# Spreading eight experts' weight loads, moving sends earlier, and regrouping the outer steps in a long convolution with routed experts

## The chip, the cores and the metric

The kernel runs on one core of one Trainium2 chip. The metric is the device time of one execution in microseconds (us), lower is better. The engines are TensorE (PE for matmuls, PEld for weight loads), VectorE (DVE), ScalarE (ACT), GpSimd (POOL) and SyncE (SP), which here issues nearly all direct DMAs and computes nothing.

## The reference

```
def _attn_ref(x, v, pos_emb, w1, w2):             # x, v: 4 x 11456 x 128
    h_filt = (np.maximum(pos_emb @ w1, 0) @ w2) * window
    y = irfft(rfft(x * v, n=2*S) * rfft(h_filt, n=2*S))[:, :S]
    return x * y
def _moe_ref(x, modality_id, w_gate, modality_bias, w1, w2):   # x: 45824 x 128
    logits = x @ w_gate + modality_bias[modality_id]           # 8 experts
    e_idx = argmax(logits); gate_w = softmax(logits)[e_idx]
    for e in range(8):                                         # w1[e]: 128 x 1024
        out[mask] = gate_w[mask] * (relu(x[mask] @ w1[e]) @ w2[e])
```

A long convolution over the sequence (by a transform of length 2S, a product, the inverse transform) is multiplied by x; each of the 45824 rows that result goes to its one best expert, a two-layer network of 128 to 1024 to 128.

## The kernel before

**Convolution and routing, about the first half of the span.** For each batch b of four there is an outer stage and a middle stage. An outer stage has 16 steps q, and each does the forward transform of a piece of batch b (`forward`, matmuls `s` of L464, copied to `A` by ACT) and, for batch b−1, the inverse transform: `turn0` and `turn1` transpose four 128x128 blocks each into PSUM twice (tile `wt`, L662), and ACT copies each `wt` out (L663); `inverse` makes `py` (L671), ACT copies half of it (L674), DVE adds, subtracts and multiplies by x. Every second step the routing of eight tokens a position goes on: `half` transposes the result (`xT`, L707), `logits` is the product with the gate (`pl`, L718), `lturn` turns that back (`lt`, L727), `biased` and `choice` find the best expert on DVE, and `send` counts the rows per expert by three matmuls (`pr`, `pn`, L785 to L790) and makes row numbers from `pr` and `pn` on DVE (L792, L793). The middle stage has 23 groups: products in the frequency domain (`pz`, L596, DVE and POOL on `part` and `more`) and inverse matmuls (`pw`, L639).

What runs in which order is a table. `OUTER` names the functions; the number behind a name is its delay in steps, and the place in the string is its order inside a step. `OV` is the number of outer steps that are interleaved with the first middle groups, `EM` says how many steps before the outer stage's end the middle stage's first step goes. PE, ACT, DVE and SP run their instructions in the order in which the program writes them; POOL's order is made by a scheduler. PSUM tiles are taken in turn: single banks (`wt`, `xT`, `pl`, `pr`, `pn`, `lt`) from four, pairs (`py`, `s1`, `pz`) from two.

**Sends.** `send_rows(1)` scatters 128 finished rows into the experts' regions of the buffer `xs` (L269, an indirect DMA on POOL). They start in the middle stages, and those of the last batch go on in the first half of the experts.

**Experts, the second half.** 82 full tiles of 512 rows in eight steps c, then half tiles of 256 rows in four steps (those beyond tile 98 lie in a branch that is skipped). Per step `hidden` is three matmuls (L1105 to L1107: high parts of weights and rows, and the two low parts), ACT's relu (L1110) and DVE's low part of it (L1111); `result` is three matmuls into `po` (L1128 to L1130), three steps late. `weights(i + 1, c)` splits the next tile's expert weights into a high part (ACT, L1064) and a low part (DVE, `wl`, L1065), in four pieces. SP's queue has, at c = 0 of tile i, `rows_in(i + 2)`: four loads of `x` (L1004), one of `ends` (gate and row number, L1006), and for tiles 0 to 7 the tile's own expert weights `w1r` and `w2r` (0.5 MB each, L1027, L1029). From tile 8 on the weights come from `w1a` and `w2a`, which hold all eight experts: 16 loads of 0.5 MB, the eight of `w1a` issued in one go in `rows_in(6)` and the eight of `w2a` in `rows_in(7)` (L1039, L1042). At the end of a tile its result goes through DRAM to change its layout: `ob<-oT` (four DMAs, L1140), then `y<-ob` (L1142), which waits for them. `rows_out` multiplies by the gate on POOL (`ot`, L1157) and scatters 128 rows at a time to `out` (L1159). `rows_turn` transposes `x` on DVE (`xT`, L1082) and casts the row numbers (`idx`, L1083), `rows_split` makes `xh` (ACT, L1091) and `xl` (DVE, L1092).

From tile 50 on the generator `rest` writes one tile of empty rows behind each expert's region (SP, `xs<-pad`, L952), each after all scatters that were issued before it, and makes the tables of the later tiles, among them those of the half tiles.

Of the kernel before, what the change touches and what calls it, by code (L numbers as in the profile page):

```python
# [12 lines left out]
F32 = mybir.dt.float32  # L13
# [8 lines left out]
ENG = mybir.EngineType  # L22
# [13 lines left out]
B, S, D, E, F = 4, 11456, 128, 8, 1024  # L36
# [4 lines left out]
NQ = N2 // 4  # L41
NO = N2 // 8
NC = 16
T = 512
# [4 lines left out]
def surely_full(n):  # L49
# [5 lines left out]
NH = (N - T * NF - E) // TH + E  # L55
RW = D + 2
NOWHERE = 1 << 20
OUTER = ("turn0:1 turn1:1 lturn:3 biased:3 forward:2 load_x:0 product:1 half:2 choice:3 "
         "inverse:1 logits:2 send:4 shift:2 load:0 store:4 places:5")
LAST = ("lturn:5 biased:5 send:6 turn0:1 choice:5 turn1:1 inverse:2 logits:4 half:3 shift:4 load_x:0 store:5 places:6")  # L60
FOUT = "load:0 hidden:2 transform:3"
FMID = "turn:0 spectrum:1 second:3"
FIRST = "forward:17 load:0 product:16"
MID = "load_c:2 spectrum:2 inverse:4 load:0"
OV, EA, EM = 2, 3, 4
F1, F2, F3 = 1, 18, 1
UNSURE = 5
TG, FL = 18, 2
NDYN = 8
# [110 lines left out]
def hyena_moe_kernel(ctx: ExitStack, tc: tile.TileContext, a: dict, out: bass.AP,  # L180
# [180 lines left out]
    with ExitStack() as cv:  # L361
# [451 lines left out]
        def outer_steps(b):  # L813

            by_block = lambda name, f: {f"{name}{k}": lambda q, k=k: f(q, k) for k in (0, 1)}
            todo = {}
            if b > 0:
                load_x, turn, itransform = inverse_stages(b - 1)
                rturn, logits, lturn, shift, biased, choice, send, store, places = route_stages(b - 1)
                todo = {  # L820
                    "load_x": load_x, **by_block("turn", turn), "inverse": itransform,
                    "half": lambda q: rturn(q // 2, q % 2), "logits": every_other(logits),
                    "lturn": every_other(lturn), "shift": every_other(shift),
                    "biased": every_other(biased),
                    "choice": every_other(choice), "send": every_other(send),
                    "store": every_other(store), "places": every_other(places)}
            if b < nb:
                load, product, transform = forward_stages(b)
                todo |= {"load": load, "product": product, "forward": transform}
            if b == nb:  # L830
                todo.pop("places")
                for name in ("half", "logits", "lturn", "biased", "choice"):
                    todo[name] = but_last(todo[name], 2)
                todo["send"] = but_last(todo["send"], 4)
                todo["store"] = but_last(todo["store"], 6)
                o = NO - 1
                finale.extend([
                    lambda late: (store(o - 2), store(o - 1), rturn(o, 0, late)),
                    lambda late: (send(o - 1), rturn(o, 1, late)), lambda late: None,
                    lambda late: logits(o, late), lambda late: None,  # L840
                    lambda late: (lturn(o), biased(o, late)), lambda late: (choice(o), store(o)),
                    lambda late: None, lambda late: (send(o), places(o))])
            table = [w.split(":") for w in (LAST if b == nb else OUTER if b else FIRST).split()]

            if 0 < b < nb:
                later.append([lambda f=todo[n]: f(NQ - 1) for n in ("store", "places")])
                todo["store"] = but_last(todo["store"], 2)
                todo.pop("places")
            return steps(NQ, [(lambda q, t=int(t): min(q + t, NQ + 3) if 0 < b < nb else q + t, todo[n])
                              for n, t in table if n in todo])  # L850

        def early(first, second, n):
# [115 lines left out]
        yield from tile_table(new, tabs["3"], took, start, left, NH, TH)  # L968

    outs, fetched = [], []  # L970
    kept = {}
    second, others = second_table(), rest()
    NCH = F // D
# [6 lines left out]
    def experts(lo, hi):  # L980
# [5 lines left out]
        def rows_in(i):  # L986
            if i > last:
                return
            tb, col, n = tiles[i]
            for gen in {"1": (), "b": (second,)}.get(tb, (second, others)):  # L990
                for _ in gen:
                    pass
            tab = tabs[tb]
            r = nc.values_load(tab[0:1, 0, col:col + 1], engines=[ENG.SP], min_val=0, max_val=E * R,
                               skip_runtime_bounds_check_because="clamped above")
            k = kept[i] = {"n": n}

            x = k["x"] = mt.tile([D, T // 32, 32], F32, tag="x", name="x", bufs=4)
            ends = k["ends"] = mt.tile([D, 4, 2], F32, tag="ends", name="ends", bufs=8)

            def rows():

                of = xs[ds(r, n), 0:D].rearrange("(f t) (k e) -> k t f e", t=32, e=32)
                lds = [sp.dma_start(x[32 * j:32 * j + 32, 0:n // 32], of[j]) for j in range(4)]  # L1004
                way = "(j p) r -> p j r" if i == last else "(p j) r -> p j r"
                lds.append(sp.dma_start(ends[:, 0:n // D],  # L1006
                                        xs[ds(r, n), D:RW].rearrange(way, j=n // D)))
                if tb in ("1", "b"):

                    known = max(nb - (2 if tb == "1" else 1), 0) * NR // D  # L1010
                    assert len(scatters) >= known
                    for ld in lds:
                        for s in scatters[known:]:
                            tc.declare_no_dep(ins_of(ld), s, reason="rows of later tiles")
                        after_all(ld, scatters[:known])

            def raw_weights():

                e = nc.values_load(tab[0:1, 2, col:col + 1], engines=[ENG.SP], min_val=0, max_val=E - 1,
                                   skip_runtime_bounds_check_because="clamped above")  # L1020
                k["w", 0] = mt.tile([D, F], F32, tag="w1r", name="w1r")
                k["w", 1] = mt.tile([D, NCH, D], F32, tag="w2r", name="w2r")
                w1 = a["moe_w1"][ds(e, 1)].rearrange("e p f -> p (e f)")
                w2 = a["moe_w2"][ds(e, 1)].rearrange("e (c p) d -> p (e c) d", p=D)
                cuts = 2 if i == 0 else 1
                cut = lambda h, n: slice(h * n // cuts, (h + 1) * n // cuts)
                return [lambda h=h: sp.dma_start(k["w", 0][:, cut(h, F)], w1[:, cut(h, F)])  # L1027
                        for h in range(cuts)] + [
                    lambda h=h: sp.dma_start(k["w", 1][:, cut(h, NCH)], w2[:, cut(h, NCH)])  # L1029
                    for h in range(cuts)]  # L1030

            of = raw_weights() if i < NDYN else []
            for part in of[:1] + [rows] + of[1:] if i == 0 else [rows] + of:
                part()
            if i < NDYN:
                k["w", 1] = k["w", 1].rearrange("p c d -> p (c d)")
            if i == min(NDYN, last) - 2:
                for e in range(E):
                    sp.dma_start(w1a[:, e], a["moe_w1"][e])  # L1039
            if i == min(NDYN, last) - 1:  # L1040
                for e in range(E):
                    sp.dma_start(w2a[:, e], a["moe_w2"][e].rearrange("(c p) d -> p c d", p=D))  # L1042

        def weights(i, part):

# [3 lines left out]
            tb, col, _ = tiles[i]  # L1049
            if part == 0 and i >= NDYN:  # L1050
                k["e"] = nc.values_load(
                    tabs[tb][0:1, 1, col:col + 1], engines=[ENG.Activation, ENG.DVE], min_val=0,
                    max_val=(E - 1) * F, skip_runtime_bounds_check_because="clamped above")
            if part % 2 == 0:
                m = part // 2
# [6 lines left out]
            else:  # L1062
                src = wv[m][:, ds(k["e"] + at, half)]
            act.copy(k[m, "h"][:, at:at + half], src)  # L1064
            dve.tensor_sub(k[m, "l"][:, at:at + half], src, k[m, "h"][:, at:at + half].bitcast(F32))  # L1065

        def turn_tiles(i):

# [6 lines left out]
        def rows_turn(i):  # L1075
# [4 lines left out]
            if "idx" not in k:  # L1080
                turn_tiles(i)
            dve.transpose(k["xT"][:, 0:n], k["x"].rearrange("p f e -> p (f e)")[:, 0:n])  # L1082
            dve.tensor_copy(k["idx"][:, 0:n // D], k["ends"][:, 0:n // D, 1])  # L1083

        def rows_split(i):
            if i > last:
# [57 lines left out]
        def rows_out(i):  # L1144
# [3 lines left out]
            n = k["n"]  # L1148
            ot = mt.tile([D, T], F32, tag="ot", name="ot", bufs=4).rearrange("p (j d) -> p j d", d=D)
            gate = k["ends"][:, 0:n // D, 0:1].broadcast_to([D, n // D, D])  # L1150
            if i == last:
                pt = bank("pt")
                for j in range(n // D):
# [17 lines left out]
        for at in range(len(work) + 6):  # L1171
# [7 lines left out]
                finale[at - FL](late)  # L1179
            if lo == 0 and at >= FL + len(finale) + 2 and len(waiting) <= RC and not fetched:  # L1180
                fetched.append(fetch(nb - 1))
            if lo == 0 and 2 * at % 7 < 2:
                send_rows(1)
            if 8 <= i < NW0:
                next(second, 0)
            if NW1 - 10 <= i < NW1:
# [2 lines left out]
                weights(i + 1, c)  # L1189
            result(at - 3)  # L1190
            whole = i <= last and tiles[i][2] == T
            if c == (3 if whole else 1):
                rows_turn(i + 1)
            if c == (4 if whole else 2):
                rows_split(i + 1)
            if c == (5 if whole else 3):
                rows_out(i - 1)
# [50 lines left out]
```

## Time and profile before

| what | value |
|---|---|
| median of 3 runs | 2198.53 us (2196.98 to 2200.67) |
| profiled execution, its own time | 2200.3 us |
| its span in the trace | 2198.5 us |
| mean granted TensorE clock | 0.985 |
| busy share: PE, PEld, DVE | 94%, 76%, 79% |
| busy share: ACT, POOL | 54%, 54% |
| queue q1 (SP's DMAs), share of 16 engines | 58.1% |

A busy PE is not a PE at its peak, since matmuls are pipelined; a stage is judged by its pitch, the time from one tile or step to the next. A wait in the trace stands in square brackets behind an instruction: the idle time just before it and what ended it. The busy shares are means over stages that have different limits, so each stage has to be read by itself.

### The profile page before, as it was taken

The numbers are of one execution on the slowest core, as the hardware profiler recorded it, in microseconds if no ns is written. First come the engines' busy times: TensorE is split into PE (matmuls) and PEld (weight loads), VectorE is DVE, ScalarE is ACT, GpSimd is POOL, SyncE is SP. The second block draws the span as 40 slices with busy tenths as digits, with TensorE's granted clock in tenths as the row PEclk, the third lists the DMA queues.
The fourth block names the chain that finished last, engine by engine and source line by source line (L and its number), as shares of the span: only waits on it lengthen the run. The fifth ranks groups of instructions, "written<-read, shape, count | busy, mean of one in ns | idle before, by whom it ended". The sixth has DMA issues, their size and how long they took to land. (4 is left out here: it accounts for less than half of the span.)

```text
span 2198.5 us, 50801 instructions
## 1 busy us (share of the span) xinstructions
PE 2076.5 (94%) x18024; PEld 1668.0 (76%) x18024; DVE 1736.2 (79%) x2946; ACT 1185.9 (54%) x2155; POOL 1186.4 (54%) x1130
## 2 busy tenths in 40 slices
PE   8989999899999999899987999999999999999985
PEld 8878776687767776687556788888888788888885
DVE  2349766896779867896895799888899899889884
ACT  4642366225652266324654566666666566666663
POOL 0216400496448855596425577777777455555533
PEclk9999999999999999999999899999999999999998
DMA  9576677678878788785678865666665555555432
GB/s 315 227 275 222 231 223 221 223 260 272 280 247 269 258 280 288 242 263 174 199 194 232 185 137 126 124 131 124 124 128 122 105 107 98 97 97 95 80 68 55
DMA packets 592748, 406.52 MB, mean 185 GB/s; under 512 B 455977, under 2 KB 489469, under 8 KB 592489
## 3 DMA queue, kind: packets, MB, share of 16 engines
q1 hardware_dynamic: 565833, 343.82, 58.1%
q0 software_dynamic: 26496, 59.36, 7.8%
q8 instruction: 144, 2.36, 0.5%
q14 instruction: 115, 0.94, 0.1%
q10 hardware_dynamic: 160, 0.03, 0.0%
HBM read 295.03 MB, written 108.42 MB: 184 GB/s over the span
## 5 line engine op out<-in xcount | busy, mean ns | idle before, releaser
L1111 DVE SCALAR_TENSOR_TENSOR hl<-ph,hh 128x512 fp32r<-128x512 f32 x724 | 485.6, 681 | 83.6 <-ACT hh L1110 76.4
L1110 ACT ACTIVATE hh<-ph 128x512 fp32r<-128x512 f32 x724 | 422.4, 597 | 203.6 <-PE ph L1107 197.1
L269 POOL DMA_INDIRECT xs<-back,to x360 | 375.8, 1044 | 279.1 <-DVE y L675 95.4
L1159 POOL DMA_INDIRECT out<-ot,idx x362 | 404.5, 1117 | 114.3 <-issue 80.2
L1107 PE MATMUL ph<-xl,wh 128*128 128x512 f32 (+1 forms) x792 | 298.4, 377 | 15.5 <-DVE xl L1092 15.5
L1128 PE MATMUL po<-hh,wh 128*128 128x512 f32 (+1 forms) x792 | 296.7, 375 | 13.4 <-ACT hh L1110 13.4
L1105 PE MATMUL ph<-xh,wh 128*128 128x512 f32 (+1 forms) x792 | 297.5, 376 | 11.1 <-ACT xh L1091 11.0
L1130 PE MATMUL po<-hl,wh 128*128 128x512 f32 (+1 forms) x792 | 296.9, 375 | 9.8 <-DVE off L316 5.1
L1106 PE MATMUL ph<-xh,wl 128*128 128x512 f32 (+1 forms) x792 | 296.7, 375 | 0.0
L1129 PE MATMUL po<-hh,wl 128*128 128x512 f32 (+1 forms) x792 | 295.7, 373 | 0.0
L643 ACT COPY A<-pw 128x512 f32<-128x512 f32 (+1 forms) x184 | 97.1, 579 | 346.3 <-PE pw L639 346.3
L1157 POOL TENSOR_TENSOR ot<-y,ends 128x512 f32<-128x512 f32 (+1 forms) x98 | 110.8, 1131 | 245.5 <-DMA y<-ob 238.0
L615 DVE TENSOR_TENSOR part<-pz,rings 128x1024 f32<-128x1024 f32 (+1 forms) x184 | 211.5, 1191 | 2.2 <-POOL part L620 2.2
L639 PE MATMUL pw<-rings,part 64*128 64x128 f32 x2880 | 201.1, 279 | 2.5 <-POOL part L620 2.5
L639 PEld LDWEIGHTS pw<-rings,part 64*128 64x128 f32 x2880 | 176.3, 188 | 35.7 <-issue 27.7
L610 POOL TENSOR_TENSOR more<-more 128x256 f32<-128x256 f32 (+1 forms) x92 | 73.0, 794 | 235.4 <-issue 150.0
L596 PE MATMUL pz<-A,rings 128*64 128x256 f32 x1440 | 176.2, 387 | 12.5 <-issue 7.3
L1107 PEld LDWEIGHTS ph<-xl,wh 128*128 128x128 f32 x792 | 151.2, 191 | 45.9 <-DVE xl L1092 20.0
L1128 PEld LDWEIGHTS po<-hh,wh 128*128 128x128 f32 x792 | 150.8, 190 | 40.8 <-ACT hh L1110 14.7
L1130 PEld LDWEIGHTS po<-hl,wh 128*128 128x128 f32 x792 | 150.6, 190 | 40.0 <-DVE hl L1111 8.8
L464 PE MATMUL s<-fwd,seq 128*64 128x90 f32 x4096 | 171.2, 242 | 9.2 <-issue 4.8
L1105 PEld LDWEIGHTS ph<-xh,wh 128*128 128x128 f32 x792 | 151.3, 191 | 37.5 <-ACT xh L1091 12.1
(180 smaller groups left out, 3720.5 us busy)
## 6 DMA issues: line engine op xcount, KB each, us to landing
rings<-hs SPq DMA_DIRECT2D x88, 512.0 KB
seq<-in_u SPq DMA_DIRECT2D x64, 512.0 KB
seq<-in_v SPq DMA_DIRECT2D x64, 512.0 KB
seq<-in_x SPq DMA_DIRECT2D x64, 512.0 KB
xr<-xo SPq DMA_DIRECT2D x64, 365.6 KB
back<-xr SPq DMA_DIRECT2D x72, 325.0 KB
rings<-in_c_b SPq DMA_DIRECT2D x88, 256.0 KB
rings<-in_c_c SPq DMA_DIRECT2D x88, 256.0 KB
```

The costliest lines, as they stand in the source:

```text
L269: s = pool.indirect_dma_start(out=xs, out_offset=bass.IndirectOffsetOnAxis(ap=ix, axis=0), in_=src, in_offset=None, bounds_check=E * R - 1 ...
L615: dve.tensor_mul(part[i], z[:, :, i].unsqueeze(1).broadcast_to([D, 2, n, 2, D]), h[:, 0].unsqueeze(3).broadcast_to([D, 2, n, 2, D]))
L639: pe.matmul(pw[par][:, to:to + D], t[at], k["c"][at, q, c], start=i == 0, stop=i == len(terms) - 1)
L1105: pe.matmul(p, k[0, "h"][:, f:f + D], k["xh"], start=True, stop=False)
L1106: pe.matmul(p, k[0, "l"][:, f:f + D], k["xh"], start=False, stop=False)
L1107: pe.matmul(p, k[0, "h"][:, f:f + D], k["xl"], start=False, stop=True)
L1110: act.activation(hh, ph, AF.Relu)
L1111: dve.scalar_tensor_tensor(hl, ph, 0.0, hh.bitcast(F32), op0=ALU.max, op1=ALU.subtract)
L1128: pe.matmul(po, k[1, "h"][:, f], hh[:, t], start=g == 0, stop=False)
L1129: pe.matmul(po, k[1, "l"][:, f], hh[:, t], start=False, stop=False)
L1130: pe.matmul(po, k[1, "h"][:, f], hl[:, t], start=False, stop=g == NCH - 1)
L1159: s = pool.indirect_dma_start(out=out, out_offset=bass.IndirectOffsetOnAxis(ap=k["idx"][:, j:j + 1], axis=0), in_=ot[:, j, :], in_offset=N ...
```

## The change

- The table `OUTER` is ordered anew and several delays grow by one; `OV` goes from 2 to 3, `EM` from 4 to 5, and the bound on late steps from NQ + 3 to NQ + 4.
- The 16 loads of `w1a` and `w2a` are issued one at a time, at odd c of tiles 2 to 5, `w1a` and `w2a` in turn.
- `send_rows(1)` is called in 3 of 10 steps where it was 2 of 7.
- The cast of `idx` moves from DVE in `rows_turn` to POOL in `rows_out`.
- In half tiles the low parts of two of the four weight pieces move from DVE to POOL, and `rows_turn` and `rows_split` come one step earlier.

```diff
-OUTER = ("turn0:1 turn1:1 lturn:3 biased:3 forward:2 load_x:0 product:1 half:2 choice:3 "
-         "inverse:1 logits:2 send:4 shift:2 load:0 store:4 places:5")
+OUTER = ("turn0:1 turn1:1 lturn:4 biased:4 send:5 half:3 forward:2 load_x:0 product:1 choice:4 "
+         "inverse:1 logits:3 shift:3 load:0 store:5 places:6")
-OV, EA, EM = 2, 3, 4
+OV, EA, EM = 3, 3, 5
...
-            if i == min(NDYN, last) - 2:
-                for e in range(E):
-                    sp.dma_start(w1a[:, e], a["moe_w1"][e])
-            if i == min(NDYN, last) - 1:
-                for e in range(E):
-                    sp.dma_start(w2a[:, e], a["moe_w2"][e].rearrange("(c p) d -> p c d", p=D))
+            if i == NDYN:
+                whole_weights(2 * E)
+
+        def whole_weights(n):
+            for _ in range(min(n, len(bulk))):
+                e, m = bulk.pop(0)
+                to, of = ((w1a[:, e], a["moe_w1"][e]) if m == 0 else
+                          (w2a[:, e], a["moe_w2"][e].rearrange("(c p) d -> p c d", p=D)))
+                sp.dma_start(to, of)
...
-            dve.tensor_sub(k[m, "l"][:, at:at + half], src, k[m, "h"][:, at:at + half].bitcast(F32))
+            eng = pool if k["n"] < T and part % 2 else dve
+            eng.tensor_sub(k[m, "l"][:, at:at + half], src, k[m, "h"][:, at:at + half].bitcast(F32))
...
-            dve.tensor_copy(k["idx"][:, 0:n // D], k["ends"][:, 0:n // D, 1])      # in rows_turn
+            pool.tensor_copy(k["idx"][:, 0:n // D], k["ends"][:, 0:n // D, 1])     # in rows_out
...
-            if lo == 0 and 2 * at % 7 < 2:
+            if lo == 0 and 3 * at % 10 < 3:
                 send_rows(1)
+            if lo == 0 and 2 <= i and c % 2:
+                whole_weights(1)
...
-            if c == (3 if whole else 1):
+            if c == (3 if whole else 0):
                 rows_turn(i + 1)
-            if c == (4 if whole else 2):
+            if c == (4 if whole else 1):
                 rows_split(i + 1)
```

On PE, in the outer stage, the second step of a pair before, from one `py` to the next (`ident` is the identity for transposes, `A` the transformed data, `oh` and `sc` the choice and its running count, `seq` the input):

```order
L671 MATMUL py<-rings,inv 64x512 x4
L718 MATMUL pl<-rings,wg 32x436 x4
L785 LDWEIGHTS both
L785 MATMUL pr<-oh_100,both 128x128
L787 LDWEIGHTS both
L787 MATMUL pr<-sc_102,both 128x128
L790 LDWEIGHTS both
L790 MATMUL pn<-sc_102,both 128x8
L662 MATMUL wt<-ident,A 90x128 x16
L727 MATMUL lt<-ident,lT 109x128 x4
L464 MATMUL s_4393<-fwd,seq 64x90 x16
L464 MATMUL s_4411<-fwd,seq 64x90 x16
```

The same step now:

```order
L671 MATMUL py<-rings,inv 64x512 x4
L662 MATMUL wt<-ident,A 90x128 x16
L785 LDWEIGHTS both
L785 MATMUL pr<-oh_100,both 128x128
L787 LDWEIGHTS both
L787 MATMUL pr<-sc_102,both 128x128
L790 LDWEIGHTS both
L790 MATMUL pn<-sc_102,both 128x8
L707 MATMUL xT<-ident,xo_88 128x109 x8
L464 MATMUL s_4374<-fwd,seq 64x90 x16
L464 MATMUL s_4392<-fwd,seq 64x90 x16
L671 MATMUL py<-rings,inv 64x512 x4
```

The three matmuls of `pr` and `pn` stood ahead of the 16 of `wt` and stand behind them now; `lt` has gone to the other step of the pair, and `xT` stands ahead of the forward matmuls.

On SP, in the first tiles of the experts, from the `ends` load of tile 6 before (`ob`, `y`: the layout change of a tile's result):

```order
L1006 DMA ends<-xs 128x4x2
L1027 ISA
L1027 DMA w1r<-in_moe_w 128x1024
L1029 ISA
L1029 DMA w2r<-in_moe_w 128x8x128
L1039 DMA w1a<-in_moe_w 128x1024 x8
L1140 DMA ob_70<-oT 32x16x32 x4
L1142 DMA y<-ob_70 128x512
```

The same queue in one of the tiles 2 to 5 now:

```order
L1007 DMA ends<-xs 128x4x2
L1028 ISA
L1028 DMA w1r<-in_moe_w 128x1024
L1030 ISA
L1030 DMA w2r<-in_moe_w 128x8x128
L1047 DMA w1a<-in_moe_w 128x1024
L1145 DMA ob_68<-oT 32x16x32 x4
L1147 DMA y<-ob_68 128x512
L1047 DMA w2a<-in_moe_w 128x8x128
L1047 DMA w1a<-in_moe_w 128x1024
L1047 DMA w2a<-in_moe_w 128x8x128
```

Eight loads in one go became four a tile, one ahead of the `ob` DMAs and three behind `y`.

On POOL, in the half tiles before, one after another:

```order
L1157 TENSOR_TENSOR ot<-y,ends 128x256
L1159 DMA out<-ot,idx 45824x128 x2
L1157 TENSOR_TENSOR ot<-y,ends 128x256
L1159 DMA out<-ot,idx 45824x128 x2
```

And now:

```order
L1163 TENSOR_TENSOR ot<-y,ends 128x256
L1071 ISA
L1071 TENSOR_TENSOR wl<-w1a,wh 128x512
L1165 DMA out<-ot,idx 45824x128 x2
L1156 CAST idx<-ends 128x2
L1071 ISA
L1071 TENSOR_TENSOR wl<-w2a,wh 128x512
L1056 TENSOR_LOAD tab_22019
```

Two `wl` pieces and the `idx` cast stand among the gate product and the scatters of a tile.

## Rows read from the trace of the kernel before

**Rows 1.** Windows: us; PE, PEld, DVE, ACT, POOL busy; granted clock; DMA share; GB/s.
```profile
1145.00:1178.00 33.00, 32.81 (x145) 27.06 (x145) 29.04 (x51) 22.39 (x42) 15.51 (x14) 1.00 0.73 174
...
1180.00:1190.00 10.00, 8.90 (x37) 6.43 (x37) 5.44 (x10) 4.14 (x8) 6.37 (x7) 1.00 0.97 317
...
2100.00:2150.00 50.00, 43.21 (x318) 41.58 (x319) 40.84 (x78) 31.07 (x59) 18.21 (x20) 0.93 0.37 69
```

**Rows 2.** Timeline of one pair of outer steps, all engines (start, duration, instruction).
```profile
305.68 2.00 PE L662 MATMUL wt<-ident,A 128*90 128x128 f32 x16
...
306.47 2.06 ACT L663 COPY rings<-wt 90x512 f32<-90x512 f32 x4
...
307.62 2.70 PE L464 MATMUL s<-fwd,seq 128*64 128x90 f32 x64
...
314.03 2.75 PE L662 MATMUL wt<-ident,A 128*90 128x128 f32 x16
...
316.34 0.28 DVE L792 TENSOR_TENSOR score<-pr,base 109x128 f32<-109x128 f32 x1
...
316.87 0.69 PE L727 MATMUL lt<-ident,lT 128*109 128x128 f32 x4
```

**Rows 3.** Timeline of PE where an outer stage passes into a middle stage.
```profile
394.00 1.46 PE L464 MATMUL s<-fwd,seq 128*64 128x90 f32 x32 [0.99 <-DVE y L677]
...
412.96 1.30 PE L596 MATMUL pz<-A,rings 128*64 128x256 f32 x10 [1.06 <-issue]
```

**Rows 4.** Groups of PE by line, 1300 to 1420 us (busy us, mean ns).
```profile
L1105 PE MATMUL ph<-xh,wh 128*128 128x512 f32 x89 | 34.6, 389 | 0.0
```

**Rows 5.** The same view, 1170 to 1290 us.
```profile
L1105 PE MATMUL ph<-xh,wh 128*128 128x512 f32 x69 | 28.0, 405 | 0.0
```

**Rows 6.** SP's DMA queue in the first tiles of the experts, and ACT's wait.
```profile
1180.88 5.77 SPq L1039 DMA_DIRECT2D w1a<-in_moe_w  x8
...
1207.79 0.62 ACT L1064 CAST wh<-w1r 128x512 fp32r<-128x512 f32 x1 [14.66 <-DMA w1r<-in_moe_w]
```

**Rows 7.** Timeline of SP's queue and POOL at the writes of empty rows.
```profile
1710.42 14.65 SPq L952 DMA_DIRECT2D xs<-pad  x5
...
1734.26 0.98 POOL L269 DMA_INDIRECT xs<-back,to  x1 [14.24 <-DMA xs<-pad]
```

**Rows 8.** Groups of PE by line, 1690 to 1770 us.
```profile
L1105 PE MATMUL ph<-xh,wh 128*128 128x512 f32 x54 | 21.5, 398 | 0.0
```

**Rows 9.** SP's DMA queue in the half tiles: first, a middle and last cycle.
```profile
2057.14 1.97 SPq L1140 DMA_DIRECT2D ob<-oT  x4
...
2116.62 1.86 SPq L1004 DMA_DIRECT2D x<-xs  x4
2118.67 0.55 SPq L1006 DMA_DIRECT2D ends<-xs  x1
2119.27 2.08 SPq L1140 DMA_DIRECT2D ob<-oT  x4
...
2164.24 1.97 SPq L1140 DMA_DIRECT2D ob<-oT  x4
```

**Rows 10.** Half tiles: PE by form, 2055 to 2165 us, and DVE by form, 2100 to 2150 us.
```profile
L1107 PE MATMUL ph<-xl,wh 128*128 128x256 f32 x119 | 35.9, 302 | 14.8 <-DVE xl L1092 14.8
...
L1065 DVE TENSOR_TENSOR wl<-w2a,wh 128x512 fp32r<-128x512 f32 x13 | 8.8, 680 | 0.1
...
L1083 DVE CAST idx<-ends 128x2 int32<-128x2 f32 x6 | 1.1, 185 | 0.7 <-DMA ends<-xs 0.7
```

**Rows 11.** POOL's groups by line, 1300 to 1650 us.
```profile
L269 POOL DMA_INDIRECT xs<-back,to x75 | 76.6, 1022 | 22.9 <-issue 22.3 <-DVE hl L1111 0.3 <-DVE wl L1065 0.3
L1157 POOL TENSOR_TENSOR ot<-y,ends 128x512 f32<-128x512 f32 x33 | 39.2, 1188 | 20.8 <-DMA y<-ob 20.6
```

**Rows 12.** Timeline of POOL and DVE at the end of the half tiles.
```profile
2163.12 0.61 POOL L1157 TENSOR_TENSOR ot<-y,ends 128x256 f32<-128x256 f32 x1 [3.68 <-DMA y<-ob]
...
2163.18 1.10 DVE L1065 TENSOR_TENSOR wl<-w1a,wh 128x512 fp32r<-128x512 f32 x1
```

More of the change, by code (lines that the diff above doesn't have):

```diff
@@ L848, in outer_steps @@
                 todo.pop("places")
-            return steps(NQ, [(lambda q, t=int(t): min(q + t, NQ + 3) if 0 < b < nb else q + t, todo[n])
+            return steps(NQ, [(lambda q, t=int(t): min(q + t, NQ + 4) if 0 < b < nb else q + t, todo[n])
                               for n, t in table if n in todo])
@@ L970, in hyena_moe_kernel @@
     outs, fetched = [], []
+    bulk = [(e, m) for e in range(E) for m in range(2)]
     kept = {}
@@ L1051, in weights @@
                 k["e"] = nc.values_load(
-                    tabs[tb][0:1, 1, col:col + 1], engines=[ENG.Activation, ENG.DVE], min_val=0,
+                    tabs[tb][0:1, 1, col:col + 1], engines=[ENG.Activation, ENG.DVE] + [ENG.Pool] * (k["n"] < T), min_val=0,
                     max_val=(E - 1) * F, skip_runtime_bounds_check_because="clamped above")
```

## The prediction

> **What bounds the kernel now.** I read the windows first, because the page's shares are means over stages with different limits, and then the stretches by groups and timelines.
>
> In the full expert tiles PE is the limit. The groups of PE by line show 89 first matmuls of L1105 in 120 us without a wait [rows 4], which is 1.35 us a step; six matmuls at their undisturbed pace make 1.36, so a tile of eight steps lasts 10.88 us. No part of the change shortens that; a gain can only come from stretches where this pace is lost. There are four.
>
> First, the outer stages. In one step of a pair the 16 transposes `wt` start at 305.68 and the next group at 307.62, after 1.94 us; in the other they start at 314.03 and the next group at 316.87, after 2.84 [rows 2]. The other step holds `pr` and `pn`, which were made just before and are not read until DVE's L792 at 316.34. They hold two of the four single PSUM banks, so the four `wt` groups share two and each waits for ACT's copy, some 0.52 us each (2.06 for four). 0.90 us is lost each time; there are six such places in each of three stages, 18 in all.
>
> Second, where an outer stage passes into a middle stage, PE waits in several places, among them 0.99 for DVE's y and 1.06 behind `pw` [rows 3]; I added up 7.4 us over each of the three passages against the groups' undisturbed times.
>
> Third, tiles 5 to 10. In 120 us there are 69 first matmuls, not 89 [rows 5]: 20 steps of 1.36 us, 27 us, are missing; by the tiles' starts 26.4. SP's queue says why: eight loads of `w1a` go out at 1180.88 and take 5.77 us to issue, and the next tile's own weights land so late that ACT stands 14.66 us [rows 6]. DMA engines are 0.97 busy there, at 317 GB/s, against 0.73 and 174 GB/s with the tiles' own weights alone [rows 1].
>
> Fourth, tiles 52 and 53. SP stands 14.65 us at five writes of empty rows, which wait for scatters issued before them, and POOL's next send 14.24 us for those writes [rows 7]; PE makes 54 steps in 80 us where 59 fit [rows 8].
>
> Then the half tiles: 119 matmuls of L1107, eight a tile, in 110 us [rows 10] are a pitch of 7.4 us, against 5.44 (half of 10.88) at PE's pace; there are sixteen such pitches. PE's wait there is put down to DVE's `xl`, 14.8 us in 110 [rows 10], and DVE is the nearly busy engine (40.84 of 50) [rows 1]. But SP's queue runs without a gap: `ends` goes out at 2118.67, is done by 2119.22, and `ob` of the next result follows at 2119.27; from 2057.14 to 2164.24 there are 14 such cycles, 7.65 us each [rows 9]. Had the result been late, SP would have stood ahead of `ob`. It stands instead between `ob` and `y`, for the write's landing. So SP's chain of small transfers sets this pitch, and DVE is late because its rows are.
>
> **The change part by part.** The sum starts from the profiled execution's own 2200.3 us (span 2198.5); the median is 1.8 us lower.
>
> *Outer order.* Nothing is added or removed. In the new order `wt` stands ahead of `pr` and `pn`, so their banks are no longer held, but two `xT` groups follow and take banks over from `wt`; ACT has y's copy of 0.6 us in front of its four `wt` copies. By those durations the last copy ends 2.85 us after the group starts, and `xT` ends 0.40 later than PE alone would have it. I take 0.90 − 0.40 = 0.5 us, × 18 = 9 us. Bounds: no stall left, 16; the same stall under another name, 0; a regrouping that starves DVE of its pairs, −9.
>
> *Passages (OV, EM).* One more outer step is laid among middle groups. The waits of 0.99 and 1.06 get other work ahead of them and go; `send`'s wait of about one for the choice stays. 7.4 falls to about 5.9, 1.5 × 3 = 4.5 us; bounds −2 to +2 each.
>
> *Weights.* The 16 loads move four tiles wide, four a tile. A load of 0.52 MB at 317 GB/s is 1.6 us at full DMA share; four make 6.4, beside the 0.73 × 10.88 = 7.9 us that a tile with its own weights takes now: 14.3 us against a pitch of 10.88, 3.4 too many in each of tiles 2 to 5, 13.8 in all. Queued behind them on SP are `x`, `ends`, `w1r` and `w2r` of the tile two ahead, whose slack is about the time between a load's landing and its use, some 3 to 4 us, and this is used up only once. So PE loses about 10 instead of 26.4: a gain of 16. Bounds: 26.4 − 13.8 less 2 or 3 for a wait of the last loads, 10; nearly all hidden, 24.
>
> *Sends.* 3 of 10 steps for 2 of 7: POOL gives out its last send in program order at tile 48, step 6, where it was tile 51, step 2. The first empty rows are written from tile 50 on, so all sends are behind them and have had about 20 us to land. Both waits of 14 us go, and with them PE's: 7.65 us by the tiles' starts, 5 steps × 1.36 = 6.8 by the counts. I take 7.6. What is next late there is nothing, since `x` then loads on time. The price is 0.114 sends more per tile, of 1.02 us and 0.3 of issue [rows 11]: 0.15 us of POOL.
>
> *idx on POOL.* No row shows such a cast on POOL. From below, DVE's takes 0.185 us [rows 10]; from above, POOL's product of 128x256 takes 0.61 [rows 12], with 0.3 between instructions. I take 0.45 in all, nearer the small cast because it has four elements a partition. In the full tiles POOL has 20.8 us of waiting for `y` in 33 tiles [rows 11], 0.63 a tile. 0.15 + 0.45 just fits: cost 0. At the upper bound POOL falls back by 0.15 + 0.91 − 0.63 = 0.43 us a tile for the 40 tiles with sends, 17 us, of which two `y` buffers hide about one tile's 10.9, so 6 would be paid. From tile 48 on sends are gone and POOL has time.
>
> *Half tiles.* DVE loses two `wl` of 0.68 and the `idx` cast, 1.55 us a tile, POOL gets them at 0.6 to 1.2 each; with `ot` and two scatters that is about 6.4 of SP's 7.65 us. Since SP's four `x`, `ends`, four `ob` and `y` are the same, I take +1 us (the first result is ready a little earlier). Bounds: −4, if a `wl` on POOL stands behind an `ot` that waits for `y` and so holds up PE; +25, below.
>
> At this place row and rule differ. The Trainium skill (Perfetto Trace Analysis, "Identifying the Most-Contended Engine") would have the engine with the highest occupancy relieved first. Here DVE's is higher than ACT's and POOL's, 40.84 of 50 [rows 1], so by that rule this is the edit that pays; the queue without gaps [rows 9] speaks against it, and that result is the second rival.
>
> A DVE `wl` of 0.68 took 1.10 us beside POOL's `ot` [rows 12]. With more work on POOL such meetings become more frequent: two or three a tile, +1 us of DVE, hidden beneath SP's 7.65. The skill (SBUF — State Buffer, "Who interferes with whom") says that a DVE instruction with two SBUF inputs contends with a GpSimd one that reads SBUF, which this row agrees with; were DVE the limit, it would take back 16 us of the rival's 25.
>
> Sum: 9 + 4.5 + 16 + 7.6 + 0 + 1 = 38.1 us. 2200.3 − 38.1 = 2162.2 by the profiled execution, 2160.4 from the median; I say 2161.
>
> **The rivals.**
> - *The stall with the weights only moves.* Loads of four a tile still delay `w1r`; every excess microsecond reaches PE and tile 8 waits for the last load. For: 14.3 against 10.88. Against: the queue is at most one load behind at a time and not eight. The gain there would be 0 to 4 instead of 16: 2161 + 14 = 2175.
> - *DVE sets the half tiles' pitch.* For: 14.8 us of PE's wait are for `xl`. Against: SP without gaps. 16 tiles × about 1.55 us: 25 more gained, 2136.
> - *POOL becomes the bound in the full tiles*, the way to slower. If the cast on POOL costs far over its bound, POOL's work a tile passes 10.88 us, `y` buffers stay full, SP stands at `y`, and `x` comes late in all the 74 tiles from 8 on. With cast and gap at 0.91 it costs 6 (2167); at 1.5 us, 0.15 + 1.5 − 0.63 = 1.02 for the 40 tiles, 41 − 11 = 30 us, and with the rest of the gain it is 2191; from about 1.8 us it is slower than before, 2200 to 2205. For: a slack of just 0.63. Against: no small instruction on any engine in these rows comes near 1.5.
> - *The outer order gives nothing or takes something*: 0 to −9 in place of 13.5: 2175 to 2184.
>
> **How the numbers follow.** Likeliest, at 2161 with its own range of 2152 to 2170: 0.62. Weights only moved: 0.12. DVE in the half tiles: 0.08. POOL the bound: 0.10, of which 0.05 slower than before. Outer order for nothing: 0.08, of which a few go with another miss. A measurement of this kernel can tell 0.2%, 4.4 us, from no change. Faster by more 0.90, within 0.04, slower by more 0.06. The range of 2148 to 2182 leaves out the DVE case and POOL's far end.
>
> **What would show it.** Outer stages: `wt` to its next group 1.94 us in both steps of a pair, a wait of 0.4 at `xT`, the first stage about 3 us shorter. Passages: no wait of about one at the forward matmuls. Weights: SP's cycles of about 14 us in tiles 2 to 5, ACT's wait for `w1r` below 6 us, tile 8 some 16 us earlier than the other gains put it. Empty rows: no wait at them above 2 us, tiles 52 and 53 at 10.88. Full tiles: POOL still waits for `y`. Half tiles: a pitch of 7.2 to 7.4, SP's cycles of 7.65, and DVE with more idle time. I am wrong if the half tiles' pitch falls below 6.6, if POOL no longer waits for `y` in tiles 9 to 47, or if ACT still waits over 10 us for `w1r`.

## The result and the profile after

The changed kernel takes 2175.52 us in the median of four runs (2170.54 to 2179.15), the kernel before 2198.36 (2196.98 to 2200.67): a ratio of 0.9894, interval 0.9872 to 0.9915. 22.8 us were gained where 38 were forecast. The whole range of 2148 to 2182 holds; the likeliest case and its own range of 2152 to 2170 missed, and the first rival's 2175 is what came. That it came so close is in part luck: the weights lost 4.8 us where that rival still had some 2 gained, and the convolution made up for it with 5 more than forecast. The profiled execution took 2179.15 us, its span 2177.3.

From the starts of the tiles (every eighth first matmul of `hidden`) the 21.2 us between the two spans divide so:

| stretch | before | after | gain | forecast |
|---|---|---|---|---|
| start to tile 0 (convolution) | 1118.6 | 1100.0 | 18.5 | 13.5 |
| tiles 0 and 1 | 27.0 | 26.3 | 0.7 | 0 |
| tiles 2 to 10 (weight loads) | 124.4 | 129.2 | -4.8 | 16 |
| tiles 52, 53 (empty rows) | 29.4 | 21.8 | 7.65 | 7.6 |
| tiles 82 to 97 (half tiles) | 116.6 | 116.5 | 0.1 | 1 |
| tile 98 to the end | 31.8 | 32.9 | -1.1 | 0 |

The other full tiles keep 10.88 us. PE's timeline of one pair of outer steps after (start, duration; the view ends in the last row's group) answers to [rows 2]:

```profile
301.41 2.00 PE L662 MATMUL wt<-ident,A 128*90 128x128 f32 x16
303.25 0.60 PE L727 MATMUL lt<-ident,lT 128*109 128x128 f32 x4
...
308.88 2.01 PE L662 MATMUL wt<-ident,A 128*90 128x128 f32 x16
310.72 0.22 PE L785 MATMUL pr<-oh,both 109*128 109x128 bf16 x1
...
311.30 1.08 PE L707 MATMUL xT<-ident,xo 109*128 109x109 f32 x8 [0.28 <-ACT rings L663]
...
317.52 0.70 PE L662 MATMUL wt<-ident,A 128*90 128x128 f32 x4
```

Both `wt` groups now take 1.84 us to the next group (301.41 to 303.25, 308.88 to 310.72); 0.43 us are lost ahead of `xT` (0.58 from `pr` to it, where `pr` and `pn` took 0.15 before). The pair lasts 16.11 us (301.41 to 317.52); it was 17.20.

SP's queue in tiles 4 and 5 after, and ACT's wait, answer to [rows 6]:

```profile
1149.58 6.14 SPq L1005 DMA_DIRECT2D x<-xs  x4
...
1156.82 0.38 SPq L1028 DMA_DIRECT2D w1r<-in_moe_w  x1
...
1158.90 3.32 SPq L1145 DMA_DIRECT2D ob<-oT  x4
1167.03 0.34 SPq L1147 DMA_DIRECT2D y<-ob  x1
...
1170.38 6.43 SPq L1005 DMA_DIRECT2D x<-xs  x4
```
```profile
1160.65 0.62 ACT L1069 CAST wh<-w1r 128x512 fp32r<-128x512 f32 x1 [10.68 <-DMA w1r<-in_moe_w]
...
1181.79 0.62 ACT L1069 CAST wh<-w1r 128x512 fp32r<-128x512 f32 x1 [12.25 <-DMA w1r<-in_moe_w]
```

A cycle of SP is 20.8 us (1149.58 to 1170.38), not 14: the four `x` loads take 6.14 us to issue, not 1.9, and `y` stands 4.8 us for `ob` to land. One wait of ACT, of 14.66 us, became three of 9.3 to 12.3; a wait over 10 us was a sign that the prediction had named for being wrong. In the windows of tiles 4 and 5 (columns as in [rows 1]) the granted clock falls:

```profile
1148.00:1168.00 20.00, 12.97 (x50) 10.00 (x50) 9.67 (x16) 7.34 (x16) 8.17 (x9) 0.83 0.85 219
1168.00:1190.50 22.50, 13.90 (x50) 10.76 (x50) 10.58 (x18) 7.85 (x15) 7.37 (x8) 0.77 0.87 227
```

The DMA engines are as full there as over the whole stretch of the two bursts before, though not as at its peak of 0.97 [rows 1]; the clock was low in that stretch too:

```profile
1178.00:1245.00 67.00, 49.20 (x184) 37.12 (x182) 36.88 (x68) 26.82 (x51) 27.76 (x26) 0.85 0.87 226
```

At the empty rows (1670 to 1750 us) PE makes all 59 steps that fit in 80 us, against [rows 8]; POOL's groups in the full tiles (1300 to 1640 us) answer to [rows 11]:

```profile
L1110 PE MATMUL ph<-xh,wh 128*128 128x512 f32 x59 | 23.0, 389 | 0.0
```
```profile
L1163 POOL TENSOR_TENSOR ot<-y,ends 128x512 f32<-128x512 f32 x31 | 34.7, 1118 | 14.1 <-DMA y<-ob 14.1
L1156 POOL CAST idx<-ends 128x4 int32<-128x4 f32 x31 | 8.3, 268 | 0.0
```

The cast takes 0.27 us there, and POOL still waits for `y`, 0.45 us a tile where it was 0.63. In the half tiles (DVE and POOL by form, 2035 to 2140 us) DVE has two pieces less and waits for `x` instead, and POOL's pieces take 1.30 us, above the 0.6 to 1.2 that I had taken, against [rows 10] and [rows 12]:

```profile
L1071 DVE TENSOR_TENSOR wl<-w2a,wh 128x512 fp32r<-128x512 f32 x14 | 15.9, 1137 | 0.3 <-ACT wh L1069 0.3
...
L1088 DVE STREAM_TRANSPOSE xT<-x 128x256 f32<-128x256 f32 x14 | 6.2, 440 | 21.6 <-DMA x<-xs 21.6
```
```profile
L1071 POOL TENSOR_TENSOR wl<-w2a,wh 128x512 fp32r<-128x512 f32 x15 | 19.5, 1302 | 2.5 <-ACT wh L1069 2.5
```

Before, DVE waited for `x` 4.8 us in 110 (2055 to 2165 us):

```profile
L1082 DVE STREAM_TRANSPOSE xT<-x 128x256 f32<-128x256 f32 x14 | 6.2, 440 | 4.8 <-DMA x<-xs 4.8
```

### The profile page after: what moved, and what is told of

It reads as the page before. It is cut to its first block, busy times and chain, and to the rows that moved or that the text cites. A ratio compares the mean times of both kernels' runs of the same rounds, so it can differ in the third digit from the quotient of the medians.

```text
span 2177.3 us, 50618 instructions
## 1 busy us (share of the span) xinstructions
PE 2053.4 (94%) x18024; PEld 1662.4 (76%) x18024; DVE 1720.4 (79%) x2813; ACT 1183.9 (54%) x2155; POOL 1236.6 (57%) x1263
## 5 line engine op out<-in xcount | busy, mean ns | idle before, releaser
L1116 DVE SCALAR_TENSOR_TENSOR hl<-ph,hh 128x512 fp32r<-128x512 f32 x724 | 480.0, 675 | 74.4 <-ACT hh L1115 67.6
L269 POOL DMA_INDIRECT xs<-back,to x360 | 369.8, 1027 | 257.9 <-DVE y L675 83.0
L1163 POOL TENSOR_TENSOR ot<-y,ends 128x512 f32<-128x512 f32 (+1 forms) x98 | 104.4, 1065 | 167.7 <-DMA y<-ob 166.7
```

The source lines that it names most:

```text
L269: s = pool.indirect_dma_start(out=xs, out_offset=bass.IndirectOffsetOnAxis(ap=ix, axis=0), in_=src, in_offset=None, bounds_check=E * R - 1 ...
L1116: dve.scalar_tensor_tensor(hl, ph, 0.0, hh.bitcast(F32), op0=ALU.max, op1=ALU.subtract)
```

## The experiments

Three sets ran on three chips, each beside the kernel before on the same chip: 2196.8 us (set a), 2201.8 (set b), 2209.7 (set c). Total times are compared within a set, and stretches by their traces. The changed kernel itself was run again in set c alone.

**a1_loads_at_once.** The two bursts again.
```diff
+            if i == min(NDYN, last) - 2: ...   # eight loads of w1a at once
+            if i == min(NDYN, last) - 1: ...   # eight of w2a
-            if lo == 0 and 2 <= i and c % 2: whole_weights(1)
```


> The changed kernel with one part undone: the 16 loads of w1a and w2a are issued as in the kernel before, eight at once in each of two tiles. Theory S (four loads a tile stretch SP's chain of x, ob, y and the tile's own weights to 20 us in four tiles running, so the spreading costs more than the two bursts did): tiles 2 to 10 take about 124 us as in the kernel before instead of 129, and the time falls by some 5 us, to about 2170. Rival B (the spreading gains as forecast and something else beside it lost the time): 16 us slower, about 2191.


Measured 2172.84 us (0.9885, 0.9865 to 0.9905); tiles 2 to 10 take 123.8 us. Rival B falls: without the spreading nothing is lost.

**a2_loads_act_queue.** `sp.dma_start(to, of)` became `act.dma_start(to, of)` in `whole_weights`.


> The changed kernel with the 16 spread loads issued by ACT, on ACT's own DMA queue, at the same places. Theory S (x, ob and y stand in one queue behind the 0.5 MB loads; they are held up by that order): the issue of the four x loads falls back from 6.1 to 2 us, y's wait for ob from 4.8 to about 2, SP's cycle from 20 to 13 to 15, tiles 2 to 10 from 129 to about 112, and the time to about 2158. Rival B (the DMA engines are full, whoever issues: 0.86 busy at 220 GB/s): cycles stay near 20 and the time within 5 us of 2175. Rival C (ACT pays for issuing): ACT loses 16 times 0.5 us among relus, 3 to 8 us more on PE.


Measured 2168.98 us (0.9869, 0.9844 to 0.9894). SP issues `x` in 1.9 to 2.6 us again, yet after one cycle of 26 us the next four are 14 to 17 us, and tiles 2 to 10 take 120.6, not 112. Order inside one queue is a part, not the main one; c3 shows that even this part is not safe. In these tiles the DMA engines have no idle time left (share 1.00, 246 GB/s), which is what rival B says of them:

```profile
1134.00:1206.00 72.00, 58.00 (x220) 43.53 (x219) 42.42 (x68) 32.37 (x61) 37.42 (x40) 0.91 1.00 246
```

**a3_loads_two_a_tile.** `NDYN = 12`, and `c % 4 == 3` for `c % 2`.


> The changed kernel with two loads a tile in tiles 2 to 9, not four in tiles 2 to 5; tiles 8 to 11 load their own weights too (NDYN 12), 4.2 MB more in all. Theory S: each load adds 10.6/4 = 2.6 us to SP's cycle of 8.3 to 13, so two a tile give 13 to 16 in the first tiles and about 11 to 13 later: PE loses 2 to 3 us in some of eight tiles, and the time is about 2160 to 2168. Rival B (what counts is the sum of bytes): the extra own weights add 4.2 MB, about 13 us of DMA time, and the time is 2175 to 2185.


Measured 2175.1 us (0.9902, 0.9878 to 0.9925). SP's cycles are 15 to 17 us in seven tiles running, and tiles 0 to 12 take 177.2. Theory S as I had put it, with cycles of 11 to 13 us, missed, and rival B's time came: these cycles have no free time for two loads a tile either.

**a4_send_behind_turns.** The old `OUTER` (OV 2, EM 4), with one function moved and its delay one longer.
```diff
-OUTER = ("turn0:1 turn1:1 lturn:3 ... logits:2 send:4 shift:2 ...")
+OUTER = ("turn0:1 turn1:1 send:5 lturn:3 ... logits:2 shift:2 ...")
```


> The changed kernel with the outer order of the kernel before (OV 2, EM 4 too), but for one function: send, which makes pr and pn, stands right behind the wt transposes. Theory of banks alone: the pair of steps goes from 17.20 to 16.1 to 16.5 us, like the changed kernel's 16.13, so the time stays within 5 us of 2175. Rival (grouping transposes with transposes and products with products is a second gain of 0.6 us a pair, since fwd takes 2.53 and not 2.63 us, wt 1.84 and not 1.94, lt 0.44 and not 0.62 when they follow a group of their own kind): the pair is 16.6 to 16.8 and the time 10 to 13 us above the changed kernel's less what the passage gives back: about 2182.


Measured 2179.19 us (0.9908, 0.9886 to 0.9929). The pair lasts 16.65 us:

```profile
303.40 2.00 PE L662 MATMUL wt<-ident,A 128*90 128x128 f32 x16
...
320.05 1.14 PE L662 MATMUL wt<-ident,A 128*90 128x128 f32 x8
```

So freeing the banks is worth 0.55 of the 1.09 us, the grouping the other 0.54. The rival holds for the pair; the total alone would not tell the two apart.

**b1_rows_before_y.** From tile 12 on, `x` and `ends` of the tile three ahead of the one at work go out between a result's `ob` and its `y`.
```diff
+                if lo == 0 and i + 4 >= NY: rows_in(i + 4)     # NY = 12
                 y = k["y"] = mt.tile(...)
...
-            if c == 0:
+            if c == 0 and (lo or i + 2 < NY):
                 rows_in(i + 2)
```


> The changed kernel with one order changed on SP, from tile 12 on: the x and ends loads of the tile three ahead stand between a result's ob and its y, so that SP issues them while ob lands and does not stand still. Theory SP (SP's chain of small transfers sets the half tiles' pitch): the cycle of about 7.65 us loses the 1.4 to 3.6 us that SP stood between ob and y, DVE no longer waits for x (21.6 us in 105), and the half tiles' 116.5 us become 98 to 107, bound then by POOL (about 6.5 us a tile) or DVE: 10 to 18 us faster than the changed kernel. Rival (compute sets the half tiles' pitch, and SP only follows it): the half tiles stay within 3 us of 116.5. Full tiles keep 10.88 us in either.


The half tiles take 109.1 us (116.5), the last eleven at a fixed 6.6. DVE waits for `x` no more, POOL is busy 83.1 of 92 us. Theory SP holds and POOL is the next limit, but the gain of 7.4 us falls short of the 98 to 107 that I expected. The time, 2195.06 us (0.9976, 0.9954 to 0.9999), shows no gain: it is that of b5, which has the old order of SP on the same chip.

**b3_rows_before_y_dve.** b1 with `dve.tensor_sub` for all pieces.


> The same as b1_rows_before_y, with all low weight parts of the half tiles on DVE as in the kernel before. If DVE is the next limit once SP isn't: DVE has 5.9 to 6.3 us of work a half tile, the 16 pitches take 96 to 104 us; against b1, where DVE and POOL slow each other (wl 0.68 to 1.14 us on DVE, 1.30 on POOL), this says which division is better: the theory that GpSimd's help is worth something expects b1 to be 5 us or more faster, the theory that the two engines' collisions eat it expects the same time or b3 faster.


Measured 2178.13 us (0.9884, 0.9861 to 0.9907), 17 us below b1; the half tiles take 96.2 us, 6.0 each. Windows and DVE by form, 2066 to 2158 us:

```profile
2066.00:2158.00 92.00, 90.29 (x735) 88.56 (x735) 89.59 (x164) 68.86 (x134) 53.51 (x61) 1.00 0.46 88
```
```profile
L1071 DVE TENSOR_TENSOR wl<-w2a,wh 128x512 fp32r<-128x512 f32 x30 | 20.1, 671 | 0.0
...
L1088 DVE STREAM_TRANSPOSE xT<-x 128x256 f32<-128x256 f32 x14 | 6.1, 435 | 0.4 <-DMA x<-xs 0.4
```

DVE is busy 89.59 of 92 us (PE is as busy, but 6.0 us a tile is above its pace of 5.44), and its `wl` takes 0.67 us again; in b1, beside POOL's, it took 1.24 to 1.34:

```profile
L1072 DVE TENSOR_TENSOR wl<-w1a,wh 128x512 fp32r<-128x512 f32 x13 | 17.4, 1340 | 0.0
```

So once SP does not set the pitch, GpSimd's share of the weights costs 13 us.

**b5_half_dve.** The changed kernel with `dve.tensor_sub` for all pieces.


> The changed kernel with one part undone: in the half tiles all low weight parts are on DVE again. Theory SP (SP's chain sets the half tiles' pitch): the same time, half tiles 114 to 118 us as now, and DVE has 6.2 us of work a tile with less waiting for x. Rival (DVE's relief paid and something else took it back): half tiles 130 to 140 us.


Measured 2194.72 us (0.9962, 0.995 to 0.9975) on set b's chip; half tiles 114.4 us. Theory SP: the move to POOL bought nothing. From here to b3, with SP's order alone changed, the half tiles gain 18.2 us and the time 16.6.

**b2_all_rows_before_y.** b1 from tile 3 on, loads from ACT's queue.


> b1_rows_before_y with the same order of SP from tile 3 on, and with the 16 loads of w1a and w2a issued by ACT on its own DMA queue. Theory S (in tiles 2 to 8 SP's chain and the DMA engines' time are both over a tile's 10.88 us; of the 16 to 20 us of SP's cycle 4.5 are its standing between ob and y): cycles of about 12 to 15 us, tiles 0 to 12 fall from 177 us (170 with ACT's queue alone) to 160 to 167. Rival (the 8.4 MB at 317 GB/s, 26.5 us, must be paid in whatever order, since nothing of the DMA time is free beside own weights): 170 or more again.


Measured 2204.85 us (1.0016, 0.9992 to 1.004): tiles 0 to 12 take 182.5 us, tiles 2 to 6 some 17 each. My theory missed altogether. As I read it, `x` and the own weights, two steps later, met the loads without any lead; no run tests that.

**c4_changed_again.** The changed kernel.


> The changed kernel itself once more, beside the others of this set: how much tiles 0 to 12 (177.2 us in its first trace, 172 to 178 in four kernels with the same code there) and the convolution vary from run to run. Theory S (spreading the loads is worth nothing, the excess of some 31 us is paid either way): tiles 0 to 12 take 172 to 178 us, as far from the 173.2 of the kernel before as the scatter. Rival (the spreading really loses 4 us): 177 again, with no value below 175.


Measured 2205.8 us (0.9979, 0.9952 to 1.0005); tiles 0 to 12 174.4. The seven traces with four loads a tile have 172.1 to 178.3 us there, mean 174.7; the two with bursts 173.2 both. On the means spreading is worth -1.5 us, within the scatter. On the two chips with traces of both it is -4.0 (177.2 against 173.2, the first chip) and -5.1 (a4 against a1), and the lower values come from the other two. It gains nothing; whether it costs stays open.

**c2_four_own_tiles.** b3 with `NDYN = 4` and the two bursts of a1.


> b3_rows_before_y_dve with four tiles that load their own weights, not eight (NDYN 4), and the 16 loads of w1a and w2a in two bursts as in the kernel before, in rows_in(2) and rows_in(3). Theory S (every load of 0.5 MB costs PE 1.6 to 2.3 us in these tiles, because SP's cycle with own weights, 12 to 13 us, is over the pitch of 10.88 already; so fewer loads is the only way to pay less): eight loads fewer, of which the tiles' slack of 2.6 us had hidden a part: tiles 0 to 12 take 163 to 168 us instead of 172 to 178. Rival (the bursts alone cost, and the own weights are hidden): 173 or more, since the bursts meet the last stores and sends of the convolution in tiles 0 and 1.


Tiles 0 to 12 take 164.2 us, within the forecast; in the windows of 1130 to 1260 us, of c2 and then of c4, PE has 118.90 us of work against 109.36:

```profile
1130.00:1260.00 130.00, 118.90 (x502) 94.63 (x499) 102.61 (x185) 71.07 (x132) 70.27 (x73) 0.95 0.77 188
```
```profile
1130.00:1260.00 130.00, 109.36 (x457) 84.47 (x456) 89.53 (x162) 65.60 (x124) 54.56 (x59) 0.93 0.82 208
```

Fewer loads pay, though the bursts also moved four tiles ahead, to tiles 2 and 3, which was not tried apart. With 2189.99 us (0.9914, 0.9885 to 0.9943) it beats both kernels on the same chip; b3's order is a part of that.

**c3_act_queue_rows_dve.** b3 with ACT's queue.


> b3_rows_before_y_dve with the 16 spread loads issued by ACT on its own queue. Tiles 0 to 12: 168 to 172 us if the 170.0 of the first kernel with ACT's queue was no accident (theory S: SP's own issue is shorter, the bytes are paid), 174 to 178 if it was. Half tiles 96 us as in b3_rows_before_y_dve.


Measured 2200.02 us (0.9957, 0.9929 to 0.9986); tiles 0 to 12 175.7, half tiles 96.7. a2's 170.0 was an accident or that chip's.

**c1_passage_as_before.** `OV, EA, EM = 2, 3, 4` with the new `OUTER`.


> The changed kernel with the new outer order, but OV 2 and EM 4 as before, so that one outer step fewer lies among middle groups. Forecast's theory (OV and EM gave 1.5 us at each of three passages): each stage, from the last pz of one middle stage to the first of the next and on to the steady groups, is 1.5 us longer than the changed kernel's. Rival (the passages did not gain, all of the outer stages' 18.5 us is from the order inside the steps): equal, or 1 to 3 us shorter a passage.


One time, 2205.07 us. From the end of the first middle stage to the end of the second, 246.1 us, against 245.8 in c4 (246.0 in the first trace after, 243.5 in a1, 251.1 before). The first outer stage is 140.1 us long in both. By this one trace OV and EM change nothing beneath the new order.

## Why the prediction was right and wrong

**Outer order: right in mechanism, mis-sized.** The stall of 0.90 us became 0.43 (forecast 0.40). But the pair gained 1.09 us, not 0.5. I had priced only the stall and held the other groups' times fixed; they depend on their neighbours. From the first to the last `wt` a stage takes 113.55 us for 121.91, 8.4 less: some 6.5 are six pairs of 1.09, the other 1.9 is work (one `pr`, `xT` and `pl`) that now lies behind the last `wt`. The order gave about 20 us in three stages, not 9.

**Passages: wrong.** "7.4 falls to about 5.9" at each: the first `wt` groups start alike, but from the last `wt` on 3.3 us of a stage's gain are given back (33.37 us to the steady groups for 30.11). Less the 1.9 of moved work, a passage costs 1.4 us where 1.5 were to be gained. c1 shows that OV and EM are worth nothing; what costs the 1.4 stays open. Both outer terms together gave 18.5, 5 more than their sum.

**Weights: the step that failed.** "14.3 us against a pitch of 10.88, 3.4 too many." I took DMA time a tile as 0.73 of PE's pitch, and the rest of the pitch as room for loads. SP, however, served no tile in 10.88 us then; successive tiles of the kernel before, without any load of `w1a` or `w2a`, show it:

```profile
1151.65 1.96 SPq L1004 DMA_DIRECT2D x<-xs  x4
...
1163.56 1.92 SPq L1004 DMA_DIRECT2D x<-xs  x4
...
1176.74 1.95 SPq L1004 DMA_DIRECT2D x<-xs  x4
```

11.9 and 13.2 us a tile with own weights alone, while PE lost nothing yet: the chain was behind already and had nothing to hide a load in. In 20 us at 0.86 the DMA engines work 17.2; in the 13.2 us their share is 0.79, which makes 10.4. So I estimate 1.7 us a load, and 2.8 us in which the engines stand idle. The price of 1.6 was near, the room was not there. What fills it is not SP's order alone, since a2 took the loads out of SP's queue and lost 23 us against PE's pace all the same, with the DMA engines full. Spread or not (a1, a3, c4), tiles 0 to 12 take 172 to 178 us; taking eight loads away (c2) gave 10.5 us against the mean of 174.7, while eight more (a3) cost 2.5, so there is no one price of a load. That is the first rival, to which I gave 0.12; its condition, 14.3 over 10.88, was in my own text.

**Empty rows: right**, 7.65 for 7.6. SP still stood 8.9 us at five of these writes, so "no wait at them above 2 us" missed; `x` came in time all the same.

**Half tiles: right.** SP's chain sets the pitch (b1, b3, b5): relieved of 1.55 us, DVE waited for `x` longer, 21.6 us in 105 for 4.8 in 110. The rule of the Trainium skill (Perfetto Trace Analysis, "Identifying the Most-Contended Engine") would have chosen DVE among the engines that it judges by occupancy, at 40.84 of 50 us [rows 1]. TensorE's rows there, 43.21 for PE and 41.58 for PEld, are higher still. Relieving DVE gave nothing (b5); with SP's order changed, where DVE is busy 89.59 of 92, relief through POOL costs 13 us (b1, b3). The other rule (SBUF — State Buffer, "Who interferes with whom") is borne out: 0.68 us became 0.96 to 1.34 beside GpSimd's pieces. That was free while SP was the limit, as I had it.

**idx on POOL and the extra sends: right**, at no cost: 0.27 us without the gap, where I took 0.45 with it.

## What to carry to other kernels

Before work is spread into a stretch, look at the cycle of the queue that must carry it, and not only at the DMA engines' busy share times another engine's pitch: a chain that takes longer than the pitch has no room. An engine that looks busiest may be waiting for rows; see whether the queue behind it ever stands idle, and try relief there first. Put loads of a later tile between a store and the load that waits for it, where they have lead: in the half tiles that gave 18.2 us, while b2, which did it in the first tiles too, took 182.5 us for tiles 0 to 12.

## What was not expected of the hardware

A group of matmuls takes longer or shorter by what stands next to it, at the same granted clock of 1.00. From start to start: 64 `s` 2.63 us between `lt` and `xT` or after `wt`, 2.53 between `xT` and `py`; four `lt` 0.62 between `wt` and `s`, 0.44 between `wt` and `xT`; 16 `wt` 1.94 ahead of `s`, 1.84 ahead of `lt`. Transposes next to transposes and products next to products save 0.54 us a pair (a4 against the changed kernel).

The changed kernel gained 22.8 us on one chip and 3.8 on set c's, where the interval takes in no gain at all. The first outer stage (last `pz` to next `pz`), without sends beside it, is 140.1 us long in all twelve traces with the new order, on every chip. The second and third are 140 to 143 us on the first chip and set a's, and 148 to 153 on those of sets b and c. The kernel before has no trace on those chips; its time is 11 us longer on set c's than on the first, the changed kernel's 30. The window 525 to 625 us, of the first trace after and of c4:

```profile
525.00:625.00 100.00, 98.26 (x1298) 74.13 (x1299) 75.18 (x154) 69.22 (x126) 51.06 (x51) 1.00 0.89 314
```
```profile
525.00:625.00 100.00, 94.10 (x1191) 67.46 (x1185) 65.14 (x130) 61.31 (x113) 48.58 (x47) 1.00 0.83 285
```

The same code does about 8% less there, at the same clock, with DMA engines less busy, and the waits are put down to "issue" or to engines that were done. Single full tiles lose some us in the same way on these chips (13 us in c4, 31 in c2), with DMA engines 0.36 busy in the longest. What holds them up stays open; the order of b1, which is in b3, c2 and c3, may have a part in the full tiles' loss, though b1 and b5, with and without it on one chip, have the same 449.1 us in tiles 11 to 51 (446.1 in the first trace after).
